# Sink transposes in the folded tile's bank, logit products behind value products, and the logits kept summed until the end

## The chip, the cores and the metric

The kernel runs on one core of one Trainium2 chip. The metric is the device time of one execution in microseconds (us), the median of three runs. The engines are named as in the profile: PE is TensorE (matrix products and transposes), DVE is VectorE, ACT is ScalarE, POOL is GpSimd, SP is SyncE, whose queue issues the DMAs. PSUM is the memory of eight banks that PE writes into; ACT and DVE read results from there.

## The reference

Three layers follow one another. An attention over 4 x 8 heads with 768 positions of width 64, in which a position sees the first 4 positions (the sinks) and the last 128 (the window). A dense layer of 3072 tokens (512 to 2048 to 512) with a gate that is 0 below -1, the identity above 1 and a parabola between. A soft mixture of 8 experts with 4 slots each.

```
scores = where(is_sink | in_window, scale * q @ k.T, -1e9)
a = softmax(scores); x = a @ v                              # (3072, 512)
h = x @ w_in
g = where(h >= 1, h, where(h <= -1, 0, (h + 1)**2 / 4))
x = g @ w_out
logits = x @ phi                                            # (3072, 32)
slot_input = softmax(logits, over tokens).T @ x
slot_out[e] = relu(slot_input[e] @ w1[e]) @ w2[e]
out = softmax(logits, over slots) @ slot_out
```

The 4 and the 128 come as data; other sizes take a second, general path of the program, which doesn't run here.

## The kernel before

The 3072 tokens are worked in 12 groups of 256. Attention runs over 96 steps m, each of two heads and 128 query positions. For each of the heads a step computes the scores (`s`, PE: two float32r products with the low parts of q and k split off, or for the first `WH` head pairs one unsplit fp32 product, line 482), the masked maximum (DVE, line 495), the exponential into p (ACT, line 502) and the norm. p holds 128 columns of one block, 16 columns of sinks and 128 columns of the next block. From step `FO` on, p is folded (line 516): both blocks are added, so that one transpose for each head suffices (`pt`, PE, line 547, into a PSUM tile with tag T), and two products on DVE (lines 554 and 555) take the parts apart again as pT. The sink columns go a way of their own: ACT and DVE write their high and low parts into sA (lines 532 and 284), PE transposes sA (`stp`, line 563) into a second tile with tag T, and ACT copies that to sTt (line 568). Tag T has two banks. `pv` (lines 578 and 587) multiplies sTt and pT of two steps by the values, in column tiles of 64; x is copied out by ACT and DVE.

The dense layer runs over 96 units n of 128 tokens and 512 hidden columns: `h` is twelve matmuls (line 622), r, a and g make the gate on ACT and DVE (lines 627, 639, 642), `gt` transposes it (`gtp`, line 648, tag T), and ACT copies it to gT (line 655). `w_out` isn't applied here; the logits come from w_out @ phi, prepared as wphi. `lg` (line 667) multiplies gT by wphi in four column tiles of 32, so that one PSUM tile holds four partial sums in its four bands of 32 partitions. For each group, DVE copies it to Lp; `lt` multiplies Lp by four stacked identities (line 679), which adds the four bands and writes the sum, logits by tokens, four times; and for each 128 tokens a 128x32 product more (line 681) gives the sum turned, tokens by logits. The first form feeds the running softmax over tokens (sm, se, et, eg, acc); the second is copied to `l_all` (line 710) for the softmax over slots at the end. eg multiplies the gate by the weights in column tiles too.

After the last group the tail follows: z and its reciprocal, u, its transpose `utp`, `ut`, the four sip steps, sip_sb (line 810), `sitp`, then the expert products w1p and w2p, whose weights are loaded meanwhile. Beside them stands the softmax over slots: cm, cx, the exponential, cz, cs and its transposes ctp.

What sets the order: a planner (`Plan`) takes every step with an engine, an estimated cost, a due time (key), dependencies and the buffers that it takes and gives back. Again and again it lets the engine that is free first take, among the steps that can start within `SLACK` of the earliest, the one with the smallest key. Each engine then works through its list strictly in that order. Keys are built from the numbers of one table (`ARATE`, `GTO`, `LGO`, `PVO`, `PTO`, `WH`, `FO`, ...). Steps whose names are in `PARTS` work in column tiles, and the planner charges a change between them and others. Where the plan leaves PE idle ahead of the first lg and behind the last h, `filled` puts in fillers: products of the identity (fill_lg, fill_S, line 1343) whose result nobody reads.

## Time and profile before

| | |
|---|---|
| median of 3 runs | 648.99 us (648.87 to 649.38) |
| the profiled execution | 649.23 us, its span 647.4 us |
| PE busy | 628.3 us, 97% of the span |
| DVE busy | 502.8 us, 78% |
| ACT busy | 418.3 us, 65% |
| DMA | 101.60 MB, 157 GB/s on average |
| largest group | h (line 622), 768 + 384 matmuls |

The program has a start in which weights are converted and PE has fillers (to about 45 us), a long middle in which attention and the dense layer run beside each other (to about 515 us, where attention ends), the rest of the dense layer (to 575 us) and the tail. Busy times of PE overlap: a matmul's row lasts until its modelled end, while the next one has long started. So in the rows of PE the distance between two starts is what a matmul takes of the engine's time.

### The profile page before, as it was taken

To read this page: it belongs to the slowest core of one execution; us is meant where nothing else is said; L and a number is where in the kernel's file an instruction comes from. 1 tells how busy PE (TensorE), PEld (TensorE's weight loads), DVE (VectorE), ACT (ScalarE), POOL (GpSimd) and SP (SyncE) were. 2 spreads that over 40 slices of the span, in tenths; PEclk is the share of its full clock that TensorE was granted. 3 is DMA by queue.
4 is the path that set the end of the run, shared out by engine and by line. 5 is a ranking of instruction groups with operands and counts; after the bars stand their busy time and mean duration, and the time that the engine had idled before them with its cause. 6 is when DMAs were issued, how large, how long until landed. Compare 5 with 4: busy or idle time off the path is not lost.

```text
span 647.4 us, 12460 instructions
## 1 busy us (share of the span) xinstructions
PE 628.3 (97%) x4471; PEld 456.5 (71%) x4471; DVE 502.8 (78%) x1568; ACT 418.3 (65%) x1181; POOL 3.3 (1%) x12
## 2 busy tenths in 40 slices
PE   8999999999999999999999999999999999999992
PEld 5667887777777778777786877777867777654452
DVE  6999999999988678788998996898998632445043
ACT  4999999997777667575665764776656533331142
POOL 0000000000000000000000000000000000010000
PEclk9999999999999999999999999999999999999997
DMA  8775583584503211422222222324230092879996
GB/s 257 239 255 164 192 267 112 195 279 138 180 27 87 71 35 34 133 65 65 67 80 82 67 68 88 87 59 151 65 97 30 23 420 104 307 308 359 423 382 217
DMA packets 34598, 101.60 MB, mean 157 GB/s; under 512 B 3808, under 2 KB 9952, under 8 KB 29920
## 3 DMA queue, kind: packets, MB, share of 16 engines
q1 hardware_dynamic: 34528, 100.73, 45.7%
q8 instruction: 37, 0.61, 0.4%
q14 instruction: 33, 0.27, 0.1%
HBM read 90.23 MB, written 10.49 MB: 156 GB/s over the span
## 4 chain that ended last, share of the span: by engine, by line
PE 68%; DVE 23%; ACT 5%; issue 1%; DMA 1%; SPq 0%; ACTq 0%; DVEq 0%
PE h L622 29%; PE gtp L648 6%; PE pv L587 5%; PE lg L667 3%; PE eg L735 3%; DVE s L495 3%; DVE kl L284 3%; PE pt L547 3%; DVE qkh L284 2%; PE s L486 2%; PE w2p L930 2%; PE w1p L892 2%; DVE gm L642 2%; PE s L482 2%; PE fill_lg L1343 2%; PE s L487 2%
## 5 line engine op out<-in xcount | busy, mean ns | idle before, releaser
L622 PE MATMUL h<-winh,x 128*128 128x512 f32 x768 | 281.0, 409 | 0.0
L622 PEld LDWEIGHTS h<-winh,x 128*128 128x128 f32 x768 | 144.3, 188 | 33.9 <-issue 7.5
L622 PE MATMUL h<-winl,x 128*128 128x512 f32 x384 | 150.2, 391 | 0.0
L502 ACT ACTIVATE p<-s,st 128x272 f32<-128x272 f32 (+1 forms) x192 | 88.0, 464 | 28.3 <-DVE st L495 27.5
L627 ACT ACTIVATE r<-h 128x512 f32<-128x512 f32 x96 | 57.3, 597 | 59.0 <-PE h L622 37.4
L495 DVE CUSTOM_DVE_ANT_0 s<-s,nm 128x272 f32<-128x272 f32 (+1 forms) x192 | 77.6, 429 | 11.4 <-PE s L487 5.8
L622 PEld LDWEIGHTS h<-winl,x 128*128 128x128 f32 x384 | 72.7, 189 | 9.0
L655 ACT ACTIVATE gT<-gtp,one 128x512 f32<-128x512 f32 x96 | 65.9, 686 | 19.0 <-PE gtp L648 18.7
L639 DVE TENSOR_SCALAR gm<-r 128x512 f32<-128x512 f32 x96 | 40.8, 427 | 36.8 <-ACT r L627 36.3
L642 DVE SCALAR_TENSOR_TENSOR gm<-r,gm 128x512 f32<-128x512 f32 x96 | 65.8, 688 | 1.3
L648 PE MATMUL gtp<-ident_r,gm 128*128 128x128 f32 x384 | 59.8, 278 | 0.4 <-DVE gm L642 0.4
L453 ACT ACTIVATE qkh<-qkr 128x672 fp32r<-128x672 f32 (+1 forms) x67 | 48.3, 728 | 12.7 <-PE s L487 12.6
L648 PEld LDWEIGHTS gtp<-ident_r,gm 128*128 128x128 f32 x384 | 44.4, 142 | 15.2 <-issue 7.9
L486 PE MATMUL s<-qkh 128*128 128x272 f32 (+1 forms) x164 | 50.3, 323 | 0.0
L587 PE MATMUL pv<-pT,v 128*64 128x128 f32 x704 | 49.0, 279 | 0.0
L284 DVE TENSOR_TENSOR kl<-qkr,qkh 128x416 fp32r<-128x416 f32 (+1 forms) x82 | 44.6, 543 | 0.8
L487 PE MATMUL s<-kl,qkh 128*128 128x272 f32 (+1 forms) x164 | 44.7, 289 | 0.4
L547 PE MATMUL pt<-ident_r,p 128*128 128x128 f32 x224 | 41.8, 280 | 0.0
L587 PEld LDWEIGHTS pv<-pT,v 128*64 128x64 f32 x704 | 37.4, 136 | 4.0 <-issue 1.0
L502 ACT ACTIVATION_READ_ACCUMULATOR p<-s,st 128x1 f32 x192 | 38.6, 201 | 0.0
L486 PEld LDWEIGHTS s<-qkh 128*128 128x128 f32 x164 | 30.9, 188 | 8.2 <-issue 6.5
L284 DVE TENSOR_TENSOR qkh<-qkr,qkh 64x256 fp32r<-64x256 f32 x82 | 34.6, 422 | 2.3
(151 smaller groups left out, 934.7 us busy)
## 6 DMA issues: line engine op xcount, KB each, us to landing
w<-in_w SPq DMA_DIRECT2D x32, 1024.0 KB, 8.6
qkr<-in_qk SPq DMA_DIRECT2D x58, 336.0 KB, 2.9
raw<-in_w_in SPq DMA_DIRECT2D x8, 1024.0 KB, 6.7
raw<-in_w_out SPq DMA_DIRECT2D x8, 1024.0 KB, 5.9
qkr<-in_qk SPq DMA_DIRECT2D x24, 264.0 KB, 2.8
v<-in_vt SPq DMA_DIRECT2D x24, 256.0 KB, 3.3
out<-o SPq DMA_DIRECT2D x12, 512.0 KB, 5.0
wo<-cv SPq DMA_DIRECT2D x8, 512.0 KB, 3.3
```

The lines of the kernel that those rows point to most:

```text
L284: V.tensor_tensor(o, x, y, ALU.subtract)
L486: T.matmul(s[:, 0:n], q, qkh[k][:, a, 256 + k0:256 + k0 + n], start=True, stop=False)
L487: T.matmul(s[:, 0:n], q, kl[k][:, a, k0:k0 + n], start=False, stop=True)
L495: V.tensor_tensor_reduce(out=s, in0=s, in1=nm, op0=ALU.add, op1=ALU.min, scale=-0.125, scalar=3.0e38, accum_out=rs[m][:, a:a + 1])
L502: A.activation(p_sb[m][:, a, 0:n], s_ps.pop((m, a))[:, 0:n], AF.Exp, bias=rs[m][:, a:a + 1], scale=-1.0, accum_out=rs[m][:, 2 + a:3 + a])
L547: T.transpose(ps[:, nc_ * a + c, :], p[:, a, col:col + 128], ident)
L587: T.matmul(ps[64 * a:64 * a + 64, t, :], vch[b, ch][:, h * 64:h * 64 + 64], o[:, len(chunks) * a + c, :], start=False, stop=(c == len(chun ...
L622: T.matmul(hps[n], x[:, c, t, :], (win_h, win_l)[w][j][:, c, :], start=(k == 0), stop=(k == 11))
L627: A.activation(r, hps.pop(n), AF.Relu, bias=0.5, scale=0.5)
L642: V.scalar_tensor_tensor(gm[n], ru.pop(n), 1.0, gm[n], ALU.subtract, ALU.mult)
L648: T.transpose(ps[:, c, :], gm[n][:, c * 128:(c + 1) * 128], ident)
L655: A.activation(gT[n // 2][:, :, t * 128:t * 128 + 128], gtp.pop(n), AF.Identity, bias=one)
```

## The change

- Sinks: from step `FO` on, the transpose of sA is written into the bank of pt, as its third tile, in one step of the planner with the two transposes of p. It waits for both p and sA, and its bank comes free when ACT has copied sTt and DVE has made pT.
- Logit products: `lg` may not be planned ahead of the pv step that `with_pv` names, and directly behind a pv its key counts as `NEAR` less. Its own due time (`LGO`) is later.
- Logits: lt loses its 128x32 products. One band of the summed form is kept in `l_sum`, 32 partitions by 256 tokens for each group, four groups above one another. At the end three steps of two transposes each (`clt`) turn it, and three copies put it in the layout of `l_all`, in the same memory.
- The table: new due times, `WH` 7 to 9, `FO` 20 to 22, `NPT` (buffers of pT and sTt) 4 to 3, and new estimated costs of some steps.

```diff
+    def near(self, e, o):
+
+        return self.NEAR if e == "PE" and self.last and self.last.name[:2] == "pv" and o.name[:2] == "lg" else 0.0
...
-                        opts.append((s, o.key, o.seq, o))
+                        opts.append((s, o.key - self.near(e, o), o.seq, o))
...
-    l_all = ct([128, 24, NS], "l_all")
+
+    l_sum = ct([128, 3, 256], "l_sum")
+    l_all = l_sum.rearrange("p b (q s) -> p (b q) s", s=NS)
...
         for a in range(2):
             for c, col in enumerate(cols):
                 T.transpose(ps[:, nc_ * a + c, :], p[:, a, col:col + 128], ident)
+        if FOLD(m):
+            st_st(m, ps[0:96, 2, :].bitcast(F32R))
         tps[m] = ps
...
-    def st_st(m):
+    def st_st(m, ps=None):
         s = sT.pop(m)
-        ps = pt([96, 128], "T", 2, nm=f"stp{m}", dt=F32R)
+        if ps is None:
+            ps = pt([96, 128], "T", 2, nm=f"stp{m}", dt=F32R)
         T.transpose(ps, s.rearrange("p a h s -> p (a h s)"), ident_r)
         sT[m] = ps
...
@@ -677,8 +688,6 @@
         n = len(SUBS[k][1])
         ps = pt([128, 512], "S" if k == LS else "lg", 2 if k == LS else 1, nm=f"lt{k}")
         T.matmul(ps[:, 0:128 * n], si128.rearrange("p a b -> p (a b)"), Lp[k][:, 0:128 * n], start=True, stop=True)
-        for t in range(n):
-            T.matmul(ps[:, 256 + 32 * t:288 + 32 * t], Lp[k][:, t * 128:t * 128 + 128], si128[:, 0, :], start=True, stop=True)
...
     def g_sm2(k):
         ps = ltp[k]
         g, ts = SUBS[k]
-        i, n = 2 * g + ts[0], len(ts)
-        V.tensor_copy(l_all[:, i:i + n, :], ps[:, 256:256 + 32 * n].rearrange("p (a b) -> p a b", a=n))
+        q, c, w = 32 * (g % 4), 128 * ts[0], 128 * len(ts)
+        V.tensor_copy(l_sum[q:q + 32, g // 4, c:c + w], ps[q:q + 32, 0:w])
...
+        def f_lt(b):
+
+            tt["clt", b] = pt([128, 2, 128], "T", 2, nm=f"clt{b}")
+            for t in range(2):
+                T.transpose(tt["clt", b][:, t, :], l_sum[:, b, t * 128:t * 128 + 128], ident)
+
+        def f_lte(b):
+            o = l_all[:, 8 * b:8 * b + 8, :].rearrange("p (q t) s -> p t q s", t=2)
+            V.tensor_copy(o, tt["clt", b].rearrange("p t (q s) -> p t q s", q=4))
...
-        s = op("cm", "DVE", .9, K + 1, lambda: f_c(0), logits)
+        lts = []
+        for b in range(3):
+            s = op(f"clt{b}", "PE", .22, K + .5, lambda b=b: f_lt(b), logits, acq=["T"])
+            lts.append(op(f"cle{b}", "DVE", .35, K + .5, lambda b=b: f_lte(b), [s], rel=["T"]))
+        s = op("cm", "DVE", .9, K + 1, lambda: f_c(0), lts)
...
-    NTW, XCAP, GCAP, RCAP, ARATE, WK0, WK1, OK0, OK1 = 7, 3, 6, 3, 0.947, -7.119, 1.613, 5.912, 1.902
-    PK0, AN0, AN1, GTO, LGO, RO, AO, PVO, PTO = 60.0, 1, 55, 2.605, 1.219, 0.818, 1.45, 0.835, 1.204
-    CKO, SPO, BO, GR, LASTN, LGT, HC, SLACK, FM = 1.82, -0.004, -0.708, 14, 5, 1.124, 6, 0.044, 0.296
-    CT0, CT1, QKR, WIK, HO, TWO, NPT, WH, FO = -1, 0.5, 3, -30, 0, 1, 4, 7, 20
+    NTW, XCAP, GCAP, RCAP, ARATE, WK0, WK1, OK0, OK1 = 7, 3, 6, 3, 0.947, -7.119, 1.613, 6.435, 1.902
+    PK0, AN0, AN1, GTO, LGO, RO, AO, PVO, PTO = 60.0, 1, 55, 2.818, 1.79, 0.87, 0.891, 1.256, 1.239
+    CKO, SPO, BO, GR, LASTN, LGT, HC, SLACK, FM = 1.633, -0.108, -0.708, 14, 5, 1.124, 6, 0.044, 0.296
+    CT0, CT1, QKR, WIK, HO, TWO, NPT, NEAR, WH = -1, 0.5, 3, -26, 0, 1, 3, 3, 9
+    FO, PAIRED, LGD = 22, 1, 1.5
...
-                    h = op(f"qh{hh}", {"ACT": .55 if wide_q else .45, "DVE": .45 if wide_q else .37}, 0, spk,
+                    h = op(f"qh{hh}", {"ACT": .64 if wide_q else .5, "DVE": .45 if wide_q else .37}, 0, spk,
                            lambda e, hh=hh: sp_hi(hh, e), [l], acq=aq, prior=[x[0] for x in sp])
-                    q = op(f"ql{hh}", "DVE", .28, spk, lambda hh=hh: sp_ql(hh), [h])
-                    kk = op(f"kl{hh}", "DVE", .46 if wide_q else .31, spk, lambda hh=hh: sp_kl(hh), [h])
+                    q = op(f"ql{hh}", "DVE", .45, spk, lambda hh=hh: sp_ql(hh), [h])
+                    kk = op(f"kl{hh}", "DVE", .6 if wide_q else .48, spk, lambda hh=hh: sp_kl(hh), [h])
...
-                q = op(f"stp{m}", "PE", .11, key + PTO + .1, lambda m=m: st_st(m), [sa], acq=["T", "sTt"], rel=["sA"])
-                sd = [op(f"ste{m}", "ACT", .16, key + PTO + .2, lambda m=m: st_ste(m), [q], rel=["T"])]
+                if not FOLD(m):
+                    q = op(f"stp{m}", "PE", .11, key + PTO + .1, lambda m=m: st_st(m), [sa], acq=["T", "sTt"], rel=["sA"])
+                    sd = [op(f"ste{m}", "ACT", .165, key + PTO + .2, lambda m=m: st_ste(m), [q], rel=["T"])]
                 nrs = [nr, sa]
             else:
                 nrs = [nr]
-            q = op(f"pt{m}", "PE", .438 if i and not FOLD(m) else .219, key + PTO, lambda m=m: st_pt(m), [nr, k_id], acq=["T", "pT"])
-            pe_ = op(f"pte{m}", "DVE" if FOLD(m) else "ACT", .78 if FOLD(m) else .49 if i else .29, key + PTO + .1, lambda m=m: st_pte(m), [q], rel=["T"])
+            if FOLD(m):
+                q = op(f"pt{m}", "PE", .28, key + PTO, lambda m=m: st_pt(m), [nr, sa, k_id], acq=["T", "pT", "sTt"], rel=["sA"])
+                sd = [op(f"ste{m}", "ACT", .165, key + PTO + .2, lambda m=m: st_ste(m), [q])]
+                pe_ = op(f"pte{m}", "DVE", .78, key + PTO + .1, lambda m=m: st_pte(m), [q])
+                op.free("T", sd + [pe_])
+            else:
+                q = op(f"pt{m}", "PE", .438 if i else .219, key + PTO, lambda m=m: st_pt(m), [nr, k_id], acq=["T", "pT"])
+                pe_ = op(f"pte{m}", "ACT", .49 if i else .29, key + PTO + .1, lambda m=m: st_pte(m), [q], rel=["T"])
...
+        def with_pv(n):
+
+            m = int((n + LGO + LGD + 10 - PVO) / ARATE) // 2 * 2 + 1
+            return [pvs[m]] if PAIRED and 0 < m < NPAIR else []
...
                 lgop[k, j] = op(f"lg{n}", "PE", .357 if last_g else .569, n + LGO, lambda n=n: u_lg(n),
                                 [gtop[n]] + ([] if last_g else [gtop[n - 1]])
                                 + ([lgop[k, j - 1]] if j else []) + ([chain] if chain and j == 0 else [])
-                                + ([att_end] if last_g else []),
+                                + ([att_end] if last_g else []), prior=with_pv(n),
                                 acq=[] if j else ["pv"] if k == LS else ["lg"], rel=["k4"] if t else [])
...
-                lt = op(f"lt{k}", "PE", .8 * h, ck, lambda k=k: g_lt(k), [lp], acq=["S" if end else "lg"], rel=["Lp"])
+                lt = op(f"lt{k}", "PE", .43 * h, ck, lambda k=k: g_lt(k), [lp], acq=["S" if end else "lg"], rel=["Lp"])
...
-                s2 = op(f"sm2_{k}", "DVE", .2, ck, lambda k=k: g_sm2(k), [se], rel=["S" if end else "lg"])
+                s2 = op(f"sm2_{k}", "DVE", .4, ck, lambda k=k: g_sm2(k), [se], rel=["S" if end else "lg"])
```

Three places show what that does to the order. In these rows a name's number tells buffers apart, x2 or x4 behind a row counts equal instructions in a row.

PE, in the middle of the program, around the lt step of the fourth group, before:

```order
L622 MATMUL h_3339<-winh_436,x_2546 128x512
L667 MATMUL lg_3131<-gT_3266,wphi 32x256 x4
L563 MATMUL stp_3362<-ident_r,sA_3329 96x128
L622 MATMUL h_3339<-winh_436,x_2546 128x512
L622 MATMUL h_3339<-winl_437,x_2546 128x512
L622 MATMUL h_3339<-winh_436,x_2546 128x512 x2
L622 MATMUL h_3339<-winl_437,x_2546 128x512
L622 MATMUL h_3339<-winh_436,x_2546 128x512
L679 MATMUL lt_3377<-Lp_3364,si_71 128x256
L681 MATMUL lt_3377<-si_71,Lp_3364 128x32 x2
L578 MATMUL pv_3386<-sTt_3306,vs_1458 128x128
```

and now:

```order
L598 MATMUL pv_3322<-pT_3305,v_5_2880 64x128 x2
L678 MATMUL lg_3066<-gT_3230,wphi 32x256 x4
L555 MATMUL pt_3351<-ident_r,p_3285 128x128 x2
L574 MATMUL pt_3351<-ident_r,sA_3333 96x128
L659 MATMUL gtp_3356<-ident_r,gm_3193 128x128 x4
L633 MATMUL h_3363<-winh_441,x_2469 128x512
L633 MATMUL h_3363<-winl_442,x_2469 128x512
L633 MATMUL h_3363<-winh_441,x_2469 128x512 x2
L633 MATMUL h_3363<-winl_442,x_2469 128x512
L633 MATMUL h_3363<-winh_441,x_2469 128x512
L690 MATMUL lt_3383<-Lp_3361,si_71 128x256
```

lg stands behind pv instead of between h and a transpose, the transpose of sA stands in the tile of pt, and lt has lost its second line.

ACT, a little earlier, around one copy of sTt, with the engines that an instruction waits for in brackets, before:

```order
L502 ACTIVATE p_3211,st_3198<-s_1_3194,st_3198 128x272 [waits DVE_49]
L507 ACTIVATE st_3198<-st_3198 128x2 [waits Activation_49]
L524 ACTIVATE p_3211<-p_3211,st_3198 128x144 [waits DVE_49]
L568 ACTIVATE sTt_3236<-stp_3226 96x128 [waits PE_49]
L532 ACTIVATE sA_3238<-p_3211 128x2x32 [waits Activation_49]
L627 ACTIVATE r_3252<-h_3203 128x512 [waits PE_49]
```

and now:

```order
L510 ACTIVATE p_3080,st_3064<-s_1_3061,st_3064 128x272 [waits DVE_49]
L515 ACTIVATE st_3064<-st_3064 128x2 [waits Activation_49]
L532 ACTIVATE p_3080<-p_3080,st_3064 128x144 [waits DVE_49]
L579 ACTIVATE sTt_3121<-pt_3103 96x128 [waits DVE_49,PE_49]
L540 ACTIVATE sA_3123<-p_3080 128x2x32 [waits Activation_49]
L638 ACTIVATE r_3129<-h_3090 128x512 [waits PE_49]
```

The copy of sTt reads pt's tile, and waits for DVE beside PE.

DVE, at the end, from acc to ut, before:

```order
L783 TENSOR_SCALAR stat<-stat 128x1
L784 RECIPROCAL stat<-stat 128x1
L744 SCALAR_TENSOR_TENSOR acc<-acc,stat,eg_7332 128x512
L726 COPY ek_7349<-etp_7339 128x32
L746 TENSOR_SCALAR acc<-acc,stat 128x512
L845 TENSOR_REDUCE cm<-l_all 128x24
L789 TENSOR_TENSOR u<-acc,eg_7352 128x512
L848 TENSOR_TENSOR l_all<-l_all,cm 128x768
L798 COPY ut<-utp 128x512
```

and now:

```order
L753 SCALAR_TENSOR_TENSOR acc<-acc,stat,eg_7213 128x512
L735 COPY ek_7231<-etp_7220 128x32
L755 TENSOR_SCALAR acc<-acc,stat 128x512
L792 TENSOR_SCALAR stat<-stat 128x1
L793 RECIPROCAL stat<-stat 128x1
L859 COPY l_sum<-clt_7225 128x2x4x32
L859 COPY l_sum<-clt_7228 128x2x4x32
L798 TENSOR_TENSOR u<-acc,eg_7234 128x512
L859 COPY l_sum<-clt_7243 128x2x4x32
L864 TENSOR_REDUCE cm<-l_sum 128x24
L807 COPY ut<-utp 128x512
```

z and its reciprocal have moved behind acc, three copies have come in, and cm stands between u and ut, where cx stood.

## Rows read from the trace of the kernel before

**Rows 1.** Stretches: window, its us; busy us (count) of PE, PEld, DVE, ACT, POOL; PEclk.

```profile
45.00:175.00 130.00, 128.98 (x893) 101.58 (x893) 126.49 (x358) 119.70 (x327) 0.00 (x0) 1.00 0.58 194
175.00:515.00 340.00, 338.09 (x2430) 255.71 (x2428) 290.08 (x959) 223.09 (x678) 0.00 (x0) 1.00 0.24 71
```

**Rows 2.** PE in order of time: start us, duration us, engine, line, names, forms, count.

```profile
266.75 0.40 PE L622 MATMUL h<-winh,x 128*128 128x512 f32 x1
266.98 0.34 PE L578 MATMUL pv<-sTt,vs 96*128 96x128 f32 x2
...
268.27 0.55 PE L648 MATMUL gtp<-ident_r,gm 128*128 128x128 f32 x3
```

**Rows 3.** PE in order of time, the second part of lt and what follows.

```profile
297.84 0.53 PE L681 MATMUL lt<-si,Lp 128*128 128x32 f32 x4
298.20 0.48 PE L622 MATMUL h<-winh,x 128*128 128x512 f32 x1
```

**Rows 4.** PE in order of time, h ahead of lg; then stp directly behind pt.

```profile
506.69 0.39 PE L622 MATMUL h<-winh,x 128*128 128x512 f32 x1
507.01 0.64 PE L667 MATMUL lg<-gT,wphi 128*32 128x256 f32 x8
...
509.16 0.30 PE L563 MATMUL stp<-ident_r,sA 128*96 128x128 f32 x1
509.30 0.45 PE L622 MATMUL h<-winh,x 128*128 128x512 f32 x1
509.59 0.39 PE L622 MATMUL h<-winl,x 128*128 128x512 f32 x1
```

**Rows 5.** PE in order of time, the first h behind an lg.

```profile
561.50 0.50 PE L622 MATMUL h<-winh,x 128*128 128x512 f32 x1
561.84 0.39 PE L622 MATMUL h<-winl,x 128*128 128x512 f32 x1
```

**Rows 6.** PE in order of time, pv with lg behind it, then a split score product.

```profile
327.21 0.34 PE L578 MATMUL pv<-sTt,vs 96*128 96x128 f32 x2
...
328.50 0.64 PE L667 MATMUL lg<-gT,wphi 128*32 128x256 f32 x8
329.07 0.39 PE L486 MATMUL s<-qkh 128*128 128x272 f32 x1
...
329.43 0.40 PE L622 MATMUL h<-winh,x 128*128 128x512 f32 x1
```

**Rows 7.** PE in order of time, two unsplit score products and the next h.

```profile
59.27 1.18 PE L482 MATMUL s<-qkr 64*128 64x272 f32 x4
60.38 0.50 PE L622 MATMUL h<-winh,x 128*128 128x512 f32 x1
```

**Rows 8.** DVE's groups: line, names, form, count; busy us, mean ns of one; idle before.

```profile
L284 DVE TENSOR_TENSOR kl<-qkr,qkh 128x416 fp32r<-128x416 f32 x58 | 34.1, 588 | 0.6
L555 DVE TENSOR_TENSOR pT<-pt,pT 128x256 f32<-128x256 f32 x64 | 27.2, 424 | 2.2
```

**Rows 9.** PE in order of time, stp between products of h.

```profile
236.46 0.22 PE L563 MATMUL stp<-ident_r,sA 128*96 128x128 f32 x1
236.52 0.45 PE L622 MATMUL h<-winh,x 128*128 128x512 f32 x1
236.80 0.39 PE L622 MATMUL h<-winl,x 128*128 128x512 f32 x1
```

**Rows 10.** PE in order of time, the first h behind pt alone.

```profile
220.69 0.48 PE L622 MATMUL h<-winh,x 128*128 128x512 f32 x1
221.00 0.40 PE L622 MATMUL h<-winl,x 128*128 128x512 f32 x1
```

**Rows 11.** DVE in order of time, at the end of the program.

```profile
583.78 0.68 DVE L789 TENSOR_TENSOR u<-acc,eg 128x512 f32<-128x512 f32 x1
...
585.24 0.68 DVE L798 COPY ut<-utp 128x512 f32<-128x512 f32 x1
...
590.29 0.75 DVE L810 TENSOR_SCALAR sip_sb<-sip,stat 128x512 f32<-128x512 f32 x1 [1.00 <-PE sip L805]
```

More of the change, by code (lines that the diff above doesn't have):

```diff
@@ L67, in setup @@
         return 0.15 if not o.name.startswith(self.PARTS) else 0.2 if o.name[:2] == "pv" else 0.0
+    NEAR = 0.0
+    def near(self, e, o):
+        return self.NEAR if e == "PE" and self.last and self.last.name[:2] == "pv" and o.name[:2] == "lg" else 0.0
     def lat(self, a, b):
@@ L1112, in fast_path @@
         cvp["pool"] = cvp["guard"].__enter__()
+        Plan.NEAR = NEAR
         plan = Plan(dict(S=2, T=2, h=2, pv=1, lg=1, qkr=QKR, qkh=2, v=4, vs=2, st=4, p=2, pT=NPT, sA=2, sTt=NPT,
@@ L1278, in fast_path @@
             aop[n] = a
-            gop[n] = op(f"g{n}", "DVE", .6, n + AO, lambda n=n: u_g(n), [a], rel=["r"])
+            gop[n] = op(f"g{n}", "DVE", .63, n + AO, lambda n=n: u_g(n), [a], rel=["r"])
             gk = n + GTO + (LGT - GTO) * max(0, 1 - (NPAIR - 1 - n) / LASTN)
```

## The prediction, made before the changed kernel ran

> **What bounds the kernel now.** I read the busy time of the engines by stage first, then PE's order of time at the places that the change touches, then DVE's groups, and last the end of the program on DVE. From 45 to 515 us PE is idle for 130 - 128.98 + 340 - 338.09 = 2.9 us in all, at the granted clock 1.00 (2.4 GHz); up to 175 us DVE (126.49 of 130 us) and ACT (119.70) are near full as well, after that they are not [rows 1]. So PE's queue sets the pace, and the change is worth what it takes out of that queue. A matmul's own duration is not its price, since matmuls overlap: the price is the distance from its start to the next start. A product of h costs 0.23 us (266.75 to 266.98 [rows 2]), though its row says 0.40.
>
> The profiled execution took 649.23 us, 647.4 of it the span; the median of three runs is 648.99, 0.24 less. I sum against the former and take 0.2 off at the end.
>
> **Shorter lt.** Before, each of the 13 lt steps has the product by Lp and one 128x32 product for each 128 tokens, two matmuls in the trace for each. Four of these take 0.36 us until the next h starts (297.84 to 298.20 [rows 3]). Eleven steps have four: 11 x 0.36 = 4.0 us gone. The copy out of lt grows on DVE from 64 to 256 columns (on 32 partitions), beside PE's products of h. The last two steps lie among fillers and count with the end. Bounds: 3.6 to 4.4.
>
> **lg behind pv.** The last h ahead of lg costs 0.32 (506.69 to 507.01 [rows 4]) and not 0.23; the first h behind lg costs 0.34 (561.50 to 561.84 [rows 5]). So a change into the narrow column tiles and back has a way in of 0.09 and a way out of 0.11 where h follows. In PE's order up to the last h I counted the unbroken stretches of column-tiled work (pv, lg, eg and phi's products): 107 before, 74 now, 23 of the new ones pv with lg behind it and nothing more. Each of the 33 that vanish saves one way in and one way out; mostly transposes followed pv, not h, so I take half of 0.11: 33 x (0.09 + 0.055) = 4.8 us. Bounds: 33 x 0.09 = 3.0 (no way out is saved) and 33 x 0.20 = 6.6.
>
> Behind pv, lg pays no way in: pv takes 1.29 us until lg starts (327.21 to 328.50 [rows 6]), and 1.29 until a transpose starts (266.98 to 268.27 [rows 2]). The Trainium skill (TensorEngine Tiling (Array Packing), Key Properties) says that a change of tiling mode drains the engine; pv's tiles are 64 columns wide and lg's 32, so by that rule pv to lg pays a way in too, and joining saves the way out alone, 1.8 us. The two equal 1.29 don't agree with it for this pair.
>
> **More whole heads.** WH goes from 7 to 9: two more head pairs, 8 score products, are done unsplit in fp32. Two of them take 1.11 us (59.27 to 60.38 [rows 7]), 0.555 each. A split one behind lg takes 0.36 (329.07 to 329.43 [rows 6]), 0.11 of that being lg's way out, so 0.25. 8 x 0.305 = +2.4 us on PE; bounds +1.6 (0.36 for a split one) to +2.6. In return DVE loses four kl at 0.59 [rows 8] and four ql, at most as much again. FO goes from 20 to 22, two pairs less are folded: four more transposes at about 0.1 (estimate, between stp's 0.06 and 0.14 below), +0.4 us on PE, and four pT products less on DVE at 0.42 [rows 8].
>
> **Sink transposes in pt's bank.** On PE I put this at 0. Apart, between products of h, stp costs 0.06 (236.46 to 236.52) and makes the next h 0.28 instead of 0.23 [rows 9]; the h behind pt alone costs 0.31 (220.69 to 221.00 [rows 10]): 0.06 + 0.05 + 0.08 = 0.19. Directly behind pt, stp costs 0.14 and the next h 0.29 [rows 4]: 0.14 + 0.06 = 0.20. 41 new pairs at 0.01 are nothing.
>
> What it costs elsewhere is the open point. In the changed order 42 of the 62 copies sTt on ACT wait for DVE, and 17 of the first pT products on DVE wait for ACT: the bank is read by one engine at a time, and two pT products take 2 x 0.42 = 0.85 us [rows 8]. So ACT can stand 0.85 us longer ahead of each such sTt, with r, gT, exp and x queued behind it, and PE waits for gT ahead of lg, and for banks that r, gT and exp set free. From below the price is 0: ACT is idle for 340 - 223 = 117 us of 175 to 515 [rows 1]. From above it is 42 x 0.85 = 36 us, if PE stood still each time. A gain of its own is possible too: 62 uses of the two T banks fall away. I take 0, the end that is nearer to the rows: all that PE waited for in that stretch, every copy of ACT included, is the 2.9 us. The planner's other numbers (due times, costs, three pT and sTt buffers for four) shift every engine's order; a better order can win PE's 2.9 us of idle time at most, a worse one is the case (c) below. That pt now waits for sB as well falls under the same range: 21 of the stp stood directly behind pt already, in an engine with 2.9 us of idle time.
>
> The Trainium skill (PSUM — Partial Sum Buffer, PSUM bank collisions raise a hardware error) says that two engines must not be in one bank and quadrant at once, two readers included. The new waits agree; this trace has no pair of engines reading one tile of that kind, so no row of it tests the rule.
>
> **Start.** The fillers ahead of the first lg fall from 60 to 51. They have h's shape; at 0.23 each 9 x 0.23 = 2.1 us gone. Bounds: 0 (PE waits for DVE or ACT instead) to 2.3.
>
> **End.** On DVE the last lt is some 0.13 shorter, and z and its reciprocal (about 0.34) move behind acc, so acc starts 0.47 earlier. Behind acc come these two and two copies of clt, priced as a 128x256 product out of pt, 0.42 each [rows 8]. In exchange cm moves behind u. It reads the same 768 columns as cx, and from u to ut, with cx between them, were 585.24 - 583.78 = 1.46 us [rows 11]; less u's own 0.6 that is about 0.86 for either. u starts at 583.78 - 0.47 + 0.34 + 0.84 - 0.86 = 583.6. Then u, the third copy and cm (0.6 + 0.42 + 0.86) stand ahead of ut: 585.5, 0.3 late. Behind ut come cx, the exponential, cs0, cz and cs1, some 0.9 + 0.85 + 0.8 + 1.4 + 0.8 (estimate: cx and the exponential at 768 columns, as cm, cz with its two small steps, cs with three), and sip_sb stands behind cs1 on DVE: 585.5 + 0.7 + 4.75 = 591.0, 0.1 more for a crossing, where it started at 590.29 after 1.00 us of idle time [rows 11]. +0.8 us for all that follows; bounds -0.1 (cs1 is hidden) and +1.3.
>
> **Sum.** -4.0 - 4.8 + 2.4 + 0.4 + 0 - 2.1 + 0.8 = -7.3. 649.2 - 7.3 = 641.9, less 0.2 for the median: 641.7 us.
>
> **Rivals.** (a) *DVE sets the pace up to 175 us.* It is 97% busy there [rows 1] and loses up to 4.7 + 1.7 us of work. If PE's late starts there come from DVE, some 4 us more goes: 637.7. Against it: PE is idle only 1.0 us in that stretch. (b) *The joined lg saves the way out alone, or PE waits at the start.* The first gives 641.7 + 3.0 = 644.7, the second 643.8, both 646.8. The rule of the tiling page would give the first. Against it: [rows 6]. (c) *ACT stands for DVE at each sTt, and PE stands for ACT.* Half of 36 us: 641.7 + 18 = 660. From 7.3 / 42 = 0.17 us for each wait the kernel is slower than before. For it: ACT takes its instructions strictly in order, and gT behind sTt frees T banks. Against it: ACT's idle time, and that PE's queue holds h products between most of what it takes from ACT. At a sixth of the price it is 648. (d) That the change doesn't do what it says is excluded by the order: the joined stretches stand in it.
>
> **How the numbers follow.** Forecast (638.5 to 644) 0.45; (a) (635 to 638.5) 0.20; (b) (644 to 647.5) 0.16; (c) mild, around 648, 0.08; (c) in earnest 0.11. The range from 635 to 648 leaves out (c) in earnest and part of its mild form. A measurement of this kernel can tell about 0.2% (1.3 us) from no change. Faster by more: 0.45 + 0.20 + 0.16 and a little of (c), 0.83; within: 0.06; slower: 0.11.
>
> **What would show it.** Right: lt without its 128x32 products; PE's idle time from 45 to 515 us still about 3 us; ACT's idle time ahead of sTt, ended by DVE, of up to 36 us, while PE waits for ACT no more than before; the last filler of the start 2 us earlier; sip_sb about 0.8 us later after the last lt. Wrong: waits of PE for gT, sTt or sA of several us (c); the last h product less than 5 us earlier (b); the stretch up to 175 us shorter by 4 us or more with DVE below 93% of it (a).

## The result and the profile after

| | us |
|---|---|
| before, median (beside the changed kernel) | 649.04 |
| changed, median of 4 runs | 642.01 (637.39 to 642.94) |
| ratio | 0.987 (95% interval 0.983 to 0.992) |
| the profiled execution of the changed kernel | 637.39, span 635.5 |

Forecast: 641.7. The kernel before varies by 0.5 us in these runs, the changed one by 5.5, and the profiled execution is the fastest of them. A fifth execution of the changed kernel, which the median leaves out, took 639.91. Against the 649.23 of before the profiled execution gains 11.8 us where the sum had 7.3. So there are two things to explain: 4.5 us that the sum has not, and what takes them away again in about half of the executions. One execution of t1 below, of 989.87 us at a granted clock of 0.56, stands in none of the figures.

The changed kernel by stage (window, its us; busy us and count of PE, PEld, DVE, ACT, POOL; PEclk, DMA share, GB/s), the answer to [rows 1]:

```profile
45.00:175.00 130.00, 130.00 (x899) 102.26 (x899) 121.68 (x338) 116.78 (x322) 0.00 (x0) 1.00 0.58 192
175.00:515.00 340.00, 339.41 (x2460) 261.15 (x2457) 297.82 (x975) 224.21 (x688) 0.00 (x0) 1.00 0.27 80
```

PE's idle time of 2.9 us has shrunk to 0.6, DVE has 4.8 us less to do up to 175 us and 7.7 more behind it.

PE in order of time where lg stands behind pv, with a joined sink transpose, the answer to [rows 6] and [rows 9]:

```profile
321.47 0.34 PE L589 MATMUL pv<-sTt,vs 96*128 96x128 f32 x2
321.73 1.09 PE L598 MATMUL pv<-pT,v 128*64 128x128 f32 x16
322.75 0.64 PE L678 MATMUL lg<-gT,wphi 128*32 128x256 f32 x8
323.32 0.44 PE L555 MATMUL pt<-ident_r,p 128*128 128x128 f32 x2
323.52 0.30 PE L574 MATMUL pt<-ident_r,sA 128*96 128x128 f32 x1
323.66 0.45 PE L633 MATMUL h<-winh,x 128*128 128x512 f32 x1
323.94 0.39 PE L633 MATMUL h<-winl,x 128*128 128x512 f32 x1
```

pv takes 1.28 until lg starts, lg 0.57, then a transpose follows. The sink's transpose takes 0.14 and the first h behind it 0.28, as priced. The form of pv's first products is full width (96*128), that of the others 64 columns.

lt in the changed kernel, the answer to [rows 3]:

```profile
176.54 0.59 PE L690 MATMUL lt<-Lp,si 128*128 128x256 f32 x2
176.97 0.38 PE L555 MATMUL pt<-ident_r,p 128*128 128x128 f32 x2
```

0.43 for the whole step.

The end on DVE, the answer to [rows 11]:

```profile
570.33 0.74 DVE L859 COPY l_sum<-clt 128x256 f32<-128x256 f32 x2
570.98 0.68 DVE L798 TENSOR_TENSOR u<-acc,eg 128x512 f32<-128x512 f32 x1
571.58 0.42 DVE L859 COPY l_sum<-clt 128x256 f32<-128x256 f32 x1
572.03 0.95 DVE L864 TENSOR_REDUCE cm<-l_sum 128x24 f32<-128x768 f32 x1
572.90 0.68 DVE L807 COPY ut<-utp 128x512 f32<-128x512 f32 x1
...
578.36 0.75 DVE L819 TENSOR_SCALAR sip_sb<-sip,stat 128x512 f32<-128x512 f32 x1
```

Copies at 0.42 and cm ahead of ut, as in the order. sip_sb has no idle time ahead of it any more (1.00 us before): DVE has become the bound there.

Between the first product of h and the first filler of the end I summed the distances from start to start on PE, by the kind of the step that begins them (us; the three traces of the changed kernel, of 637.39, 638.36 and 638.41 us, have 532.6, 533.1 and 533.7 in all):

| | before | changed | x1 | x4 | x3 | x5 | b_wh9 | t1 |
|---|---|---|---|---|---|---|---|---|
| h | 284.7 | 280.0 | 280.3 | 280.7 | 282.5 | 281.2 | 285.2 | 284.6 |
| s, unsplit | 8.2 | 12.7 | 12.8 | 12.7 | 12.8 | 8.3 | 12.6 | 8.6 |
| s, split | 50.8 | 44.5 | 44.1 | 47.1 | 44.7 | 47.2 | 46.9 | 49.0 |
| pt and stp | 27.3 | 29.8 | 30.0 | 30.5 | 29.4 | 30.4 | 28.1 | 28.7 |
| pv | 56.9 | 57.3 | 57.2 | 57.0 | 56.5 | 57.2 | 56.8 | 58.1 |
| lg | 26.8 | 26.6 | 26.7 | 26.7 | 26.9 | 26.8 | 26.8 | 26.9 |
| lt | 9.0 | 4.3 | 8.8 | 4.3 | 4.5 | 4.3 | 8.8 | 4.1 |
| gtp | 38.8 | 37.1 | 37.2 | 37.1 | 38.4 | 38.6 | 38.5 | 37.3 |
| fillers | 5.1 | 3.5 | 3.4 | 3.5 | 3.4 | 7.1 | 5.1 | 8.8 |
| others | 37.4 | 36.9 | 36.9 | 36.9 | 36.7 | 38.0 | 37.9 | 37.6 |
| all | 545.1 | 532.6 | 537.3 | 536.5 | 535.8 | 539.0 | 546.7 | 543.5 |

The columns from x1 on are the experiments below, where their names stand in brackets. The first h starts at 29.9 us before and at 29.6 to 30.2 in the three traces; the end, from the first filler there to w1p, has grown from 17.6 to 18.4; behind w1p both take 54.8. So in these executions the whole gain of 11.8 us, and 0.8 more, lies between the first h and the end.

### The profile page after: what moved, and what is told of

It is laid out like the page before. It is cut to its first block, busy times and chain, and to the rows that moved or that the text cites. A ratio compares the mean times of both kernels' runs of the same rounds, so it can differ in the third digit from the quotient of the medians.

```text
span 635.5 us, 12324 instructions
## 1 busy us (share of the span) xinstructions
PE 616.9 (97%) x4420; PEld 453.3 (71%) x4420; DVE 502.3 (79%) x1561; ACT 412.3 (65%) x1175; POOL 3.3 (1%) x12
## 4 chain that ended last, share of the span: by engine, by line
## 5 line engine op out<-in xcount | busy, mean ns | idle before, releaser
L461 ACT ACTIVATE qkh<-qkr 128x672 fp32r<-128x672 f32 (+1 forms) x61 | 44.0, 729 | 15.9 <-PE s L495 15.9
L494 PE MATMUL s<-qkh 128*128 128x272 f32 (+1 forms) x156 | 46.9, 318 | 0.2 <-ACT p L510 0.2
L292 DVE TENSOR_TENSOR kl<-qkr,qkh 128x416 fp32r<-128x416 f32 (+1 forms) x78 | 42.2, 541 | 0.6
L495 PE MATMUL s<-kl,qkh 128*128 128x272 f32 (+1 forms) x156 | 42.1, 287 | 0.0
L510 ACT ACTIVATION_READ_ACCUMULATOR p<-s,st 128x1 f32 x192 | 38.6, 201 | 0.0
L555 PEld LDWEIGHTS pt<-ident_r,p 128*128 128x128 f32 x228 | 28.4, 141 | 12.3 <-issue 3.7
L494 PEld LDWEIGHTS s<-qkh 128*128 128x128 f32 x156 | 29.4, 189 | 10.6 <-issue 8.4
```

The costliest lines, as they stand in the source:

```text
L292: V.tensor_tensor(o, x, y, ALU.subtract)
L461: A.activation(h[:, i, 0:w], qkr[hh][:, 0:w], AF.Copy)
L494: T.matmul(s[:, 0:n], q, qkh[k][:, a, 256 + k0:256 + k0 + n], start=True, stop=False)
L510: A.activation(p_sb[m][:, a, 0:n], s_ps.pop((m, a))[:, 0:n], AF.Exp, bias=rs[m][:, a:a + 1], scale=-1.0, accum_out=rs[m][:, 2 + a:3 + a])
L555: T.transpose(ps[:, nc_ * a + c, :], p[:, a, col:col + 128], ident)
```

## The experiments

Times are the median of 4 to 12 executions in five rounds, with their lowest and highest; ratios are to the kernel before, measured beside them. Each trace is of one execution.

### Each term by itself

The products of lt, put back in the changed kernel's own order (x1):

```diff
         T.matmul(ps[:, 0:128 * n], si128.rearrange("p a b -> p (a b)"), Lp[k][:, 0:128 * n], start=True, stop=True)
+        for t in range(n):
+            T.matmul(ps[:, 256 + 32 * t:288 + 32 * t], Lp[k][:, t * 128:t * 128 + 128], si128[:, 0, :], start=True, stop=True)
```

> The changed kernel in its own order on every engine, with the 128x32 products of lt put back behind the 128x256 one; nothing reads what they write. Theory: they stand in PE's queue and nothing hides them, so 11 steps by 0.36 us come back: 642.0 + 4.0 = 646.0, 645 to 647. Rival: PE waits for others often enough that 4 us of extra products are taken out of its waits: 642 to 643.

644.14 us (642.65 to 649.28), ratio 0.993 (0.990 to 0.995). The stretch from the first h is 537.3, 4.2 longer than the mean of the three, and lt itself 4.5 (8.8 for 4.3): nothing hides these products. That the median is only 1 us above that of the changed kernel measured beside it (643.09) is the start's doing, below: there five of the changed kernel's six executions had a granted clock of 0.992 or less. At equal clock the times agree with the stretch. The four executions of x1 at 0.993 took 642.65 to 644.24, the seven of the changed kernel at 0.993 or 0.994 took 637.39 to 639.91, and their medians are 4.8 apart.

lg parted from pv by six products of h (x2; the text of `apart` is left out here and below):

```diff
-        order = plan.run()
+        order = apart(plan.run())   # the next h step is set ahead of lg, 23 times
```

> The changed kernel with the next six products of h taken ahead of lg in 23 of the 26 places in which lg stands directly behind pv; all else in the same order on every engine. There are 97 unbroken stretches of column-tiled work for 74. Theory: each parting brings one way out behind pv (0.11 us) and one way in ahead of lg (0.09): 23 x 0.20 = 4.6, so 646.6, 645.5 to 647.5. Rival, by which pv to lg is a change of tiles with its own price: only the way out comes back, 23 x 0.11 = 2.5, 644.5. Second rival: the joining saves nothing, 642.

663.41 us (660.59 to 663.48), ratio 1.021 (1.019 to 1.023): 20 us more than the changed kernel, none of the readings. In some 19 of the 23 places a score product or a transpose stood between lg and that h, and it came 1.4 us later too. Who waited for whom in it (us, times, longest):

```profile
PE pv L589 <- ACT sTt L579: 2.2, 5, 1.0
PE pt L574 <- DVE sA L292: 1.8, 5, 0.4
PE s L494 <- ACT p L510: 1.4, 3, 0.5
PE lt L690 <- DVE Lp L684: 1.1, 2, 0.6
PE etp L729 <- DVE l_sum L719: 1.1, 2, 0.6
```

No one wait is large, but from 175 to 515 us PE's busy time falls to 331.06 of 340. The experiment moved more than it meant to, so I parted them again, by the one step that follows lg (x4):

```diff
-        order = plan.run()
+        order = apart(plan)   # the step behind lg is set ahead of it, 22 times
```

> The changed kernel with the one step that follows lg on PE (a score product, a transpose or h) taken ahead of lg, in 22 of 26 places in which lg stands directly behind pv: as the kernel with six products of h between, but no other step is moved behind those products. 96 stretches of column-tiled work for 74. Theory: 22 x (0.09 way in + 0.06 to 0.11 way out) = 3.3 to 4.4 us in the stretch from the last filler of the start to the first filler of the end, so 519 becomes 522.5 to 523.5, and the time 645 to 647; the 16 us of the former kernel came from scores and transposes that came 1.4 us later behind the six products, and are gone. Rival: the parting itself costs 0.9 us each, by a price that the rows don't show; then the stretch is again some 539 us and the time above 660.

644.89 us (640.81 to 645.82), ratio 0.993 (0.991 to 0.995). The stretch is 536.5, 3.4 more than the mean of the three: 22 x 0.155. One of its places:

```profile
324.07 0.44 PE L555 MATMUL pt<-ident_r,p 128*128 128x128 f32 x2
324.27 0.29 PE L574 MATMUL pt<-ident_r,sA 128*96 128x128 f32 x1
324.50 0.64 PE L678 MATMUL lg<-gT,wphi 128*32 128x256 f32 x8
325.06 0.50 PE L633 MATMUL h<-winh,x 128*128 128x512 f32 x1
325.40 0.40 PE L633 MATMUL h<-winl,x 128*128 128x512 f32 x1
```

The sink's transpose takes 0.23 here, ahead of lg, and 0.14 above, ahead of h; the first h takes 0.34 behind lg and 0.28 above. Summed over the 22 places alone, against the mean of the three traces, the parting costs 3.9 us, mostly 0.15 to 0.20 each. So it costs what the rows of before said, and the other 16 us of x2 are put down, by the difference of the two kernels, to steps that came late for ACT and DVE.

Sinks in a tile of their own again (x3; more lines of the two steps change with them):

```diff
-        if FOLD(m):
-            st_st(m, ps[0:96, 2, :].bitcast(F32R))
...
-                q = op(f"pt{m}", "PE", .28, key + PTO, lambda m=m: st_pt(m), [nr, sa, k_id], acq=["T", "pT", "sTt"], rel=["sA"])
...
+                q = op(f"pt{m}", "PE", .219, key + PTO, lambda m=m: st_pt(m), [nr, k_id], acq=["T", "pT"])
...
```

> The changed kernel with the transpose of sA in a tile and a planner's step of its own again, as in the kernel before; the planner makes a new order (84 stretches of column-tiled work for 74). Theory: the joining itself is worth nothing, ten more stretches cost 10 x 0.145 = 1.5: 643.5, 642 to 645. Rival (c) of the prediction in mild form: the joining holds ACT behind DVE at the copies of sTt and PE behind ACT; without it the time falls to 640 or less, with fewer waits of PE in the trace. Third reading: the joining frees T banks and so takes waits from PE; then 646 or more, with more waits of PE for sTt, gT or pT.

642.10 us (641.83 to 643.58), ratio 0.989 (0.987 to 0.990). The stretch is 535.8, and 1.7 of that is a fall of the clock just behind the first h (below). What is left, 534.1, is 1.0 more than the mean of the three, where ten more stretches of column-tiled work would cost 1.6 (eight by the widths in the rows, 1.2). So the joined bank is worth nothing within some 0.6 us, either way, as far as a kernel can show it whose whole order is a new one. ACT's wait for it is real, though; in the changed kernel, ahead of the copies of sTt (us, times):

```profile
L579 ACT ACTIVATE sTt<-pt x62: 255/273/277, 117.8 to 503.3; 96x128 fp32r<-96x128 f32 x62
...
its engine sat idle before it (us, times) until:
  DVE pT L565: 11.8, 20
  DVE st L519: 6.4, 9
```

In x3 there are none that DVE ends, but 11.0 us for PE's stp. PE stood for sTt 0.2 us in the changed kernel, as in x3.

### Whole heads

In the changed kernel WH back to 7 (x5), and in the kernel before WH 9 and FO 18 (b_wh9):

```diff
-    CT0, CT1, QKR, WIK, HO, TWO, NPT, NEAR, WH = -1, 0.5, 3, -26, 0, 1, 3, 3, 9
+    CT0, CT1, QKR, WIK, HO, TWO, NPT, NEAR, WH = -1, 0.5, 3, -26, 0, 1, 3, 3, 7
```

```diff
-    CT0, CT1, QKR, WIK, HO, TWO, NPT, WH, FO = -1, 0.5, 3, -30, 0, 1, 4, 7, 20
+    CT0, CT1, QKR, WIK, HO, TWO, NPT, WH, FO = -1, 0.5, 3, -30, 0, 1, 4, 9, 18
```

> The changed kernel with WH 7 as before, so that two head pairs more are split into high and low parts: 4 ql and 4 kl more on DVE, 8 unsplit score products of 0.57 us become split ones of 0.25 to 0.31; a new order (80 stretches for 74). Theory of the prediction's sum: PE gets shorter by 2.0 to 2.5, six stretches cost 0.9, the stretch from the last filler of the start to the first of the end falls from 519 to about 517.5, and PE's stalls in it stay at 4 us. Rival (a) of the prediction: DVE sets PE's pace up to 175 us, and its relief took 4 us of stalls away; then DVE is 96% busy there again (93.6% in the changed kernel) and the stretch is 521 us or more.

> The kernel before with WH 9 for 7 and FO 18 for 20, nothing else (with FO 20 its planner finds no order): two head pairs more unsplit, two more folded; 105 stretches of column-tiled work for 107. Theory of the prediction's sum: +2.4 for the unsplit products and -0.4 for the folding on PE: 651.4, 650.5 to 652. Rival (a), which the changed kernel and its version with WH 7 speak for: the relief of DVE and ACT up to 175 us takes away more waits than the products cost; then the stalls of PE from 65 to 195 us (5.6 to 6.5 us in the kernel before) fall to 2, and the time is 645 to 648.5.

x5 took 647.25 us (642.23 to 650.54), ratio 0.996 (0.994 to 0.998), b_wh9 652.16 (650.66 to 659.25), ratio 1.007 (1.005 to 1.009). They don't agree on rival (a). In the kernel before, more whole heads cost 1.6 us in the stretch of the trace, near the sum's +2.0. By the medians they cost 3.1 (652.16 for the 649.07 beside it): that trace is of the second fastest of eleven executions, and what the others lose is not shown. In the changed kernel, fewer of them cost 4.2 as well (539.0 less 1.7 for the clock, against 533.1). The table shows most of where: unsplit products 4.4 less, split ones 2.7 more, but fillers 7.1 for 3.5, 27 of them behind the first h for 13, and gtp 1.5 more. Fillers stand where the plan leaves PE idle up to the first lg, at 105 to 117 us; DVE and ACT are near full there (57.5 and 58.3 of 60 us from 45 to 105 in x5), and the trace calls PE busy. So it seems that what whole heads are worth depends on whether the plan can use what they free: not in the order of before, where 19 fillers stay 19.

### Code or table

The changed kernel's code with the table of before (t1):

```diff
...
-    PK0, AN0, AN1, GTO, LGO, RO, AO, PVO, PTO = 60.0, 1, 55, 2.818, 1.79, 0.87, 0.891, 1.256, 1.239
+    PK0, AN0, AN1, GTO, LGO, RO, AO, PVO, PTO = 60.0, 1, 55, 2.605, 1.219, 0.818, 1.45, 0.835, 1.204
...
-    CT0, CT1, QKR, WIK, HO, TWO, NPT, NEAR, WH = -1, 0.5, 3, -26, 0, 1, 3, 3, 9
-    FO, PAIRED, LGD = 22, 1, 1.5
+    CT0, CT1, QKR, WIK, HO, TWO, NPT, NEAR, WH = -1, 0.5, 3, -30, 0, 1, 4, 0, 7
+    FO, PAIRED, LGD = 20, 0, 1.5
```

> The code of the changed kernel with the table of the kernel before: its due times, WH 7, FO 20, NPT 4, and lg not tied to pv (PAIRED 0, NEAR 0); the planner's new costs stay. The sinks share pt's bank, lt has no 128x32 products, the logits are turned at the end. 98 stretches of column-tiled work, for 107 before and 74 in the changed kernel. Theory: only the terms of the sum count: lt -4.0 to -4.5, nine stretches -1.3, the end +0.9, the sinks 0; 649.1 becomes 644 to 645, and PE's stalls between the last filler of the start and the first of the end fall little, from 11 us to 9 or 10. So the other 3 to 6 us of the changed kernel come with its table: lg behind pv, and an order with fewer stalls. Rival 1: the code itself (the bank freed, the shorter lt) takes the stalls away; then 641 or less, with stalls of 5. Rival 2: the old due times don't suit the new steps; then 647 or more.

650.44 us (647.31 to 656.96), ratio 1.002 (0.999 to 1.005): no gain, where rival 2 had 647 or more. The trace is of an execution of 647.87. lt has lost its 4.9 us there too, and split scores and gtp 3.3, but fillers take 8.8 us, 33 of them behind the first h, pv 1.2 more, pt and stp 1.4. The stretch is 1.6 us shorter than before, and the end gives half of that back. The other eight executions, of 649.7 or more, had a granted clock of 0.991 or less; the three at 0.994 took 647.31 to 648.43. So what the code is worth with this table is 1 to 2 us at the full clock, and nothing in the median. My 644 to 645 left the fillers out, and the nine stretches: by the widths in the rows there are 107 as before, since lg often stands ahead of pv, which opens at full width. With the old table the time that the code frees goes into fillers.

### The spread

The changed kernel twice more (a1 and a2):

> The changed kernel once more, unedited, in five rounds. Its four times lie between 637.39 and 642.94 us, a spread of 5.5, where the kernel before has 0.5; the one trace there is belongs to the fastest. Theory: the sum over PE's queue gives some 642, and the median is 642 again, 641 to 643. What differs between its runs is to be read from a second trace, if it falls on another time. Reading 1: PE waits more for ACT and DVE in the middle in the slower runs; then the last product of h comes 3 to 5 us later in a slower trace, with the end unchanged. Reading 2: the weights of the experts or the output arrive late; then the last h is at the same time within 1 us and the stretch behind sip_sb is longer.

> The changed kernel once more, unedited, beside the two others of this call, for a third trace and more times. Theory: its time is set by its start. Traces of the same order of the start so far have the first filler at full rate at 13.6 to 14.0 us, the first product of h at 29.3 to 30.2 and then 636 to 639 us of span, or the first fast filler at 15.0 to 15.5 and the first h at 31.7 to 33.0. So in a trace of 637 to 640 us the first h comes at 29 to 30.5, in one of 641 to 645 at 31.5 to 34, and the stretch from the first h to the first filler of the end is 532 to 535 in either. Rival: the slower runs lose their time behind the first h; then that stretch is 536 or more with an early first h.

Medians 643.09 (638.36 to 645.20) and 638.83 (638.35 to 644.54), ratios 0.991 (0.990 to 0.993) and 0.987 (0.984 to 0.990). All seventeen times of the changed kernel fall into two groups: eight from 637.4 to 639.9 and nine from 641.3 to 645.2. The granted clock of a whole execution is 0.992 to 0.994 in the eight and 0.982 to 0.992 in the nine. All three traces are of the first group; in them the first h comes at 29.6 to 30.2 us and the stretch behind it is 532.6 to 533.7, as expected of early starts; no trace fell on a slower time, so the other half of that expectation stays untested. x1 has the same order up to the first lt, at 176 us, and its trace shows the other kind of start. PE's fillers and the score products that wait, in the changed kernel:

```profile
11.86 1.20 PE L1380 MATMUL fill_lg<-ident_r 128*128 128x512 f32 x2
...
13.65 1.66 PE L1380 MATMUL fill_lg<-ident_r 128*128 128x512 f32 x6
...
28.43 0.48 PE L490 MATMUL s<-qkr 64*128 64x128 f32 x2
28.85 0.96 PE L1380 MATMUL fill_lg<-ident_r 128*128 128x512 f32 x3
29.64 0.40 PE L633 MATMUL h<-winh,x 128*128 128x512 f32 x1
```

and in x1:

```profile
13.66 2.51 PE L1382 MATMUL fill_lg<-ident_r 128*128 128x512 f32 x6
...
30.48 0.46 PE L490 MATMUL s<-qkr 64*128 64x128 f32 x2 [1.12 <-DMA qkr<-in_qk]
30.87 0.96 PE L1382 MATMUL fill_lg<-ident_r 128*128 128x512 f32 x3
31.67 0.39 PE L633 MATMUL h<-winh,x 128*128 128x512 f32 x1
```

The six fillers take 0.9 us more in x1: PE goes over from 0.43 us for a filler to 0.22 later (at 15.5 us, in the changed kernel at 14.0). All that PE feeds is then 0.9 late, among it the release of two buffers of q and k. Their loads go out at 23.9 and not 23.0, and land 6.6 us later instead of 5.4: PE waits, and the first h is 2.0 us late. Late landing doesn't need the late change of rate, though: in a1 the fillers were fast from 13.9 us, the loads took 6.2 and PE waited 0.6, in a2 they were fast from 14.0 and the loads took 3.3. In x3 and x5 those loads took 7.5 and 7.8 us, PE waited 2.1 and 2.3, and behind that the clock fell. x3 (columns as above):

```profile
28.00:32.00 4.00, 1.74 (x7) 1.18 (x8) 3.27 (x11) 2.98 (x9) 0.00 (x0) 1.00 0.95 279
32.00:36.00 4.00, 4.00 (x14) 2.97 (x13) 1.97 (x5) 1.90 (x9) 0.00 (x0) 0.57 0.08 29
```

A granted clock of 0.57 over four us is 1.7 us of PE's work, and the first h products there cost 0.42 each. Spread over 640 us it is 0.003, the distance of 0.991 from 0.994. So a late start alone, as in x1, would take the changed kernel's fast times to some 639.5 to 641; the nine, at 641.3 to 645.2, have lost clock as well, by their figures. In the kernel before the loads took 3.9 us and PE did not wait; its score product stands some 0.6 us later.

Three kernels try to mend it: loads of q and k earlier by a fourth buffer (q4), eight more fillers ahead of the waiting product (x7), and five more ahead with the three behind it taken away (x8).

```diff
-    CT0, CT1, QKR, WIK, HO, TWO, NPT, NEAR, WH = -1, 0.5, 3, -26, 0, 1, 3, 3, 9
+    CT0, CT1, QKR, WIK, HO, TWO, NPT, NEAR, WH = -1, 0.5, 4, -26, 0, 1, 3, 3, 9
```

> The changed kernel with four buffers for the raw q and k (QKR 4 for 3), so that the loads of the ninth and following heads are issued earlier in the start; the planner makes a new order (82 stretches for 74). What it tests: in six traces so far, two loads of q and k are issued at about 23 us and land 3.9 us later in the kernel before, but 5.4 to 7.5 us later in the changed kernel and its variants, and PE waits for the second at 28 us, up to 2.1 us, after which the granted clock fell to 0.57 for four us in one trace; the last filler of the start lies between 43.0 and 47.2. Theory: this makes the spread of the changed kernel (637.4 to 645.2) and raises its median; with the loads earlier the wait goes, the last filler comes at 44 or earlier (eight more fillers, about 1.8 us, stand there), the spread falls to 2 us, the clock is 0.993 or more in all runs and the median is 638 to 640. Rival: the spread comes from elsewhere (the end, DVE and ACT in the middle); then it stays at 5 us and the median at 642 to 643.

```diff
             n = int((o.start - t - FM) / cost) if a else 0
+            if o.name == "s6_1":
+                n += 8
```

> The changed kernel in its own order with eight more fillers (some 1.8 us) directly ahead of the score product that waits for a load of q and k at 28 us. Theory: in slower runs PE stands there 1 to 2.3 us, and behind it the granted clock fell to 0.57 for four us; fillers keep PE busy, so the clock stays up: all runs at a clock of 0.993 or more, times between 639 and 643 with a median of 641, the fastest 1 to 2 us slower than the fastest of the changed kernel. Rival: the clock's fall has nothing to do with that wait or costs nothing; then the spread stays 5 us and all is 1 to 2 us slower, median 643 to 645.

```diff
             n = int((o.start - t - FM) / cost) if a else 0
+            if o.name in ("s6_1", "h0_0"):
+                n = n + 5 if o.name == "s6_1" else 0
```

> The changed kernel with the three fillers that stand behind the waiting score product of the start, at 28 us, and the one two places later set ahead of it, and two more: six ahead of it for one, none behind it. All else in the same order. It should keep PE busy for the load of q and k at no price where the load is early. Theory: the fastest runs at 638 to 639.5, as in the changed kernel, the slowest at 641.5 to 642 for 645, the median at 639 to 641. Rival: the score product that comes later moves DVE and ACT back, which are full there; then it costs what eight more fillers cost, fastest 640, median 641 or more.

The fourth buffer did not help: 644.61 (640.40 to 648.84), ratio 0.992 (0.989 to 0.995), six of its times at 642.5 or less and six at 646.8 or more. That wait is gone, but in its trace (646.4 of span) PE still ran at its slow rate at 22 us (twelve products of pv in 1.55 us, 0.88 in the changed kernel), and the first h came at 32.4. The eight fillers: 641.31 (640.20 to 641.82), ratio 0.988 (0.986 to 0.990); the spread fell to 1.6 us, as expected, and the fastest got 2 us slower; but two of the five clocks are 0.991, not 0.993 or more. The moved fillers: 638.76 (638.20 to 641.13), ratio 0.984 (0.982 to 0.985), the lowest of all, and all five clocks are 0.993 or 0.994. Its trace is of the longest of the five, 641.13:

```profile
28.30 1.66 PE L1380 MATMUL fill_lg<-ident_r 128*128 128x512 f32 x6
...
31.95 0.46 PE L490 MATMUL s<-qkr 64*128 64x128 f32 x2 [1.98 <-DMA qkr<-in_qk]
32.33 0.50 PE L633 MATMUL h<-winh,x 128*128 128x512 f32 x1
```

```profile
28.00:32.00 4.00, 2.02 (x9) 1.31 (x9) 2.64 (x8) 1.67 (x6) 0.00 (x0) 1.00 0.97 266
32.00:36.00 4.00, 4.00 (x19) 2.93 (x20) 3.21 (x11) 4.00 (x11) 0.00 (x0) 1.00 0.12 47
```

The loads took 8.6 us, longer than in any other trace, though the fillers were fast from 14.3 us; PE still waited 2.0 us, but the clock stayed at 1.00. That is one trace, and the wait was a little shorter than the 2.1 and 2.3 of x3 and x5. Since a2, the kernel unmended, had a median of 638.83, the five times of x8 alone don't show that its start is better. It is faster than the kernel before beyond doubt, than the changed kernel by likelihood only.

## Why the prediction was right, and which steps were not

The median came out 0.3 us from the forecast, but not by the sum's way, and the closeness is luck: measured again, the same kernel had medians of 643.09 and 638.83.

- **lt**: -4.0 forecast, -4.5 by x1, on PE's path as said.
- **lg behind pv**: 33 x 0.145 = 4.8 forecast; x4 gives 0.155 for each by the stretch, 0.18 by its places. By the widths in PE's rows 28 changes fell away and not 33 (107 to 79), since lg or eg ahead of pv joins nothing: 4.3 to 5.0. The price was right, its reason not: that pv takes 1.28 until lg and 1.29 until a transpose [rows 2] doesn't mean that lg pays nothing. From pair to pair inside pv there are 0.10 us, from its last product to whatever follows 0.20, lg included. By the Trainium skill's rule (TensorEngine Tiling (Array Packing), Key Properties: a change of tiling mode drains the engine) pv to lg is such a change, and these 0.10 us agree with it. What does not hold is the 1.8 us that the prediction made of the rule: parting brings back the way in (0.09 ahead of lg) and the slower first product behind it (0.05 to 0.10) too.
- **Sinks**: 0 forecast, 0 within 0.6 us by x3. Rival (c) was right in its mechanism and wrong in its price: ACT did stand for DVE, 18 us in 29 places, while PE stood 0.2 us for sTt and 0.6 us in all from 45 to 515. ACT had the idle time that [rows 1] show. In the trace no copy of sTt overlaps a read of pt by DVE, as the Trainium skill wants it (PSUM — Partial Sum Buffer, PSUM bank collisions raise a hardware error); no run tried what happens otherwise.
- **Whole heads and folding**: +2.8 forecast. With the folding the other way, +1.6 in the trace of b_wh9 for a forecast of +2.0, so the price on PE is about right; its median, +3.1, has 1.5 us more that no trace shows. What was missing is that whole heads can buy fewer fillers (x5).
- **PE's idle time**: I took 2.9 us as all that PE could win. That step was wrong: fillers hid another 5.1 us behind the first h, and waits hide in the modelled ends of the matmuls. To size them I took PE's runs of products of one kind (h in sixes, gtp and lg in fours) and summed what each distance has above the lower quartile for as many between the same neighbours (before, changed and b_wh9 taken together, last filler of the start to first of the end): 11.2 us before, 7.2 to 8.2 in the three traces of the changed kernel, 10.1 in b_wh9. That is 3 to 4 us that the sum has not, 2 to 3 of them up to 175 us (4.3 before, 1.0 to 2.0 now). It came with the whole table, and no experiment here takes one number of it apart from the rest, so its cause stays open. Rival (a) named DVE up to 175 us as its place and 4 us as its size. Place and size fit, and DVE's share there fell to 93.6%. But its relief alone does not do it. In b_wh9 DVE is 95.1% busy there and in t1 93.3%, less than in the changed kernel, and neither gains these us (b_wh9, then t1, columns as above):

```profile
45.00:175.00 130.00, 128.52 (x871) 99.91 (x869) 123.69 (x351) 116.17 (x317) 0.00 (x0) 1.00 0.57 188
45.00:175.00 130.00, 128.42 (x872) 99.54 (x871) 121.27 (x334) 116.00 (x312) 0.00 (x0) 1.00 0.57 186
```

- **Start**: -2.1 forecast. In the early starts the first h is 0.3 earlier to 0.3 later and six of the nine missing fillers stood behind it (-1.6); in the late ones it is some 2 to 3 us later in the traces of its variants, with the fall of the clock on top in x3 and x5. The last filler of the start came 0.8 to 1.3 us earlier, not 2. I had the bound "PE waits for DVE or ACT instead" but did not look at the loads of q and k, on which it waits.
- **End**: +0.8 forecast, +0.8 measured, with DVE as the bound ahead of sip_sb.

So the sum was 4 us short in the middle, and the late starts, with the clock that they lose, take about as much away: an error of the middle and one of the start cancelled in the median. Where the start is early the kernel lies at 637.4 to 639.9, six times of eight nearer to rival (a)'s 637.7 than to the forecast. That the nine slower times of the changed kernel itself are late starts is inferred from x1, x3 and x5 and from their lower clock; no trace of the unedited kernel in that group was taken.

## What to carry to other kernels

Price a step on a full engine from start to start and it holds within a tenth or two, as lt, lg and the end did; but count fillers as idle time, and expect a new order to win or lose some us more than its terms. Time that the code frees is a gain only where the order of the other engines can use it: the same code with the old table gained nothing in the median. When a kernel's spread grows after a change, compare the granted clocks of its executions and the start of traces of different times before reading anything into a median. Fillers ahead of a wait, rather than behind it, are worth a try; x8 speaks for it and doesn't show it.

## What the runs showed of the hardware

- PE's products take twice as long at first: 0.43 us for a filler, and 0.22 from a moment on that differs between executions of one order, 13.6 to 15.6 us, and 27.0 in the trace of q4, which has another order. The column PEclk shows 1.00 all through.
- Behind a wait of PE of 2.1 and 2.3 us for a load the granted clock was 0.57 on average over four us, so most of that time at the lower of its two levels (1.2 and 2.4 GHz), and an h product cost 0.42 us for 0.23. Behind a wait of 2.0 us with six fillers ahead of it (x8) it stayed at 1.00; whether by the fillers or by the shorter wait is open.
- The same two loads of 132 and 168 KB took from 3.3 (a2 and b_wh9) to 8.6 us (x8) to land, issued 3 to 4 us behind a load of 1 MB.
- A change of width costs PE time at both sides. In the changed kernel the last 64-column product of pv stands 0.20 us ahead of a 32-column lg, of a transpose and of a score alike, for 0.10 between two pairs inside pv; h stands 0.33 ahead of lg for 0.23, a score 0.22 for 0.13; and the first score product behind pv or lg takes 0.23 for 0.13.
- Scores and transposes that came 1.4 us late at some 19 places went with 16 us more (x2 less x4): it seems that the engines that wait for PE had no such slack.
